# Small inputs spread over 128 partitions, w_out read in 8-KB runs, and the engines' work lists written anew

## The chip, the cores and the metric

The kernel runs on one core of one Trainium2 chip. The metric is the device time of one execution in microseconds (us). Before the change seven executions gave a median of 246.35 us, from 245.91 to 246.79. A measurement of this kernel can tell about 0.2% (0.5 us) from no change.

## The reference: what is computed

Inputs are q, k and v with 8 batches, 8 heads, 576 rows and 64 columns, p with 32 rows instead of 576, and the weights w_in (512 x 2048), w_out (2048 x 512) and beta (2048), all fp32.

```
sm_attn(q, k, v) = softmax(q k^T / 8) v
p_packed = sm_attn(p, k, v)              # 32 rows per head
x = sm_attn(q, p_packed, p_packed)       # 576 rows per head; heads side by side: 4608 x 512
h = x @ w_in                             # 4608 x 2048
out = (h * sigmoid(beta * h)) @ w_out    # 4608 x 512
```

## The kernel before

**The work.** Each batch b passes through two stages. The attention stage transposes k and q, forms the scores of p against k (`s1`, `s1r`), their exponentials (`e1`) and sums (`z1`), and the packed values `pp`. The second attention is never multiplied out: `scaled_w` (line 793, the instruction in 798) forms W = (pp times w_in) times 1/sum times beta, 128 rows by 2048 columns in two halves r, and the second attention's weights A2 (`s2`, `e2`, `z2`, `l2`, `n2`, `A2`) multiply W directly. The MLP stage forms h(b, ft) = W A2 for 16 blocks ft of 128 hidden columns (`main`), takes Silu on ScalarE (`g`), and multiplies by w_out (`o` tasks, in batches 0 and 1 plainly, from batch 2 on with seven products of half size, `p` and `P`). Because Silu is taken of beta times h, w_out is divided by beta row by row when it is cast to bf16 (`cast_out`, line 1276, tasks `w_out`).

**The layout that the change touches.** Hidden column f sits in block ft = f // 128 on partition f % 128. So w_out is loaded as `(f p) n -> p f n` (`load_out`, line 1270): for each of 128 partitions four rows of 2 KB, a quarter of w_out (1 MB) per load, four loads `ld_out` 0 to 3. beta is loaded as 16 rows of 128 (`load_beta`, 1143), made safe against division by zero (`safe`, 1220), transposed to a column per block (`column`, task `bcol`), inverted (`rbeta`), and spread to all partitions with fp32 matmuls (`spread`, tasks `brow`, then `beta`). p of batches 0 and 1 is loaded with 32 rows on 32 partitions (`load_first`, 1148), cast, transposed in four pieces (`first_transpose`, 1159) and placed; p of the other six batches is loaded later on 96 partitions (`load_p`, 1151), doubled and transposed (`transpose`, 1191; `place`, 1200).

**The order.** Nothing is scheduled when the program runs. `SEQUENCE` (line 54) lists, for TensorE (PE), ScalarE (ACT), VectorE (DVE), GpSimd (POOL) and SyncE (SP), the tasks in the order in which each engine issues them; every engine works through its own list and waits where an input is not there. `Planner.run` walks the five lists with an estimate for each task. The estimates move no task, but from them `fill` (in `run`) decides how many small matmuls without use (`keep_warm`, tile `o_ps<-identr`) stand in a place where PE is expected to wait during the first 60 us. SP issues nearly all the copies. In its list the loads of batches 0 and 1 and of the weights stand in one row, and each of the three staging buffers of w_in and w_out has to be cast before it is loaded again.

The places that the prediction's steps touch are these. `("o", 0, 1, 13)` is in both versions the first product that reads the last quarter of w_out; it needs `w_out` 12 and 13. Before it PE's list has

```
("s2", 0, 1), ("s2", 1, 0), ("o", 0, 1, 9), ("z2", 0, 2), ("o", 0, 0, 9), ("w", 1, 0), ("o", 0, 0, 11),
("z2", 1, 0), ("o", 0, 1, 11), ("o", 0, 1, 13), ("z2", 1, 1), ...
```

## Time and profile before

| what | value |
|---|---|
| median of 7 executions | 246.35 us |
| the profiled execution | 245.62 us, of which its span is 243.8 us |
| PE busy | 229.5 us (94%), 2432 matmuls, of them 147 without use (13.2 us) |
| ACT busy | 174.8 us (72%) |
| DVE busy | 153.7 us (63%) |
| POOL busy | 60.3 us (25%) |
| granted TensorE clock | 0.999 |
| DMA | 54.13 MB in 74986 packets, mean 222 GB/s |

The span runs from the first to the last recorded instruction of the core; 1.8 us of the execution lie around it. All times below that are given as points (51.37 us, say) are counted from the start of the span. A line of the timeline gives start, length, engine, source line, operation and tiles, and in brackets the idle time before it with what ended it. In the chain of work that ended last, each piece is followed back to what released it.

### The profile page before, as it was taken

What the parts mean: (1) busy time and instruction counts of PE and PEld (TensorE: products, weight loads), DVE (VectorE), ACT (ScalarE), POOL (GpSimd) and SP (SyncE); (2) the same over time, 40 slices, a digit from 0 to 9 for tenths busy, and PEclk for the clock granted to TensorE, in tenths of its full rate; (3) what the DMA queues carried; (4) which work ended last, traced back from release to release, by engine and by line L of the source; (5) the groups of instructions that cost most, each with busy time, mean ns of one, the idle gap of its engine ahead of it and who ended that gap; (6) DMA issues with size and microseconds to landing.
All of it is one profiled execution on the core that took longest, in us unless ns stands there. A gap on an engine that the chain in (4) does not pass through costs nothing.

```text
span 243.8 us, 5850 instructions
## 1 busy us (share of the span) xinstructions
PE 229.5 (94%) x2432; PEld 153.3 (63%) x2460; DVE 153.7 (63%) x244; ACT 174.8 (72%) x311; POOL 60.3 (25%) x77
## 2 busy tenths in 40 slices
PE   3997889989999999999999999999999999999994
PEld 3985545534464444687578754876588655767893
DVE  5445966879946636993798447845895158912721
ACT  2355969787797997797578866998798769866210
POOL 6422001125443065018520452036006000000000
PEclk9999999999999999999999999999999999999999
DMA  6999999999999999999999996998991530006033
GB/s 178 323 335 322 340 377 322 368 255 320 235 242 188 279 290 266 228 290 309 238 221 267 305 176 165 264 314 234 193 291 42 114 151 4 0 0 218 0 110 107
DMA packets 74986, 54.13 MB, mean 222 GB/s; under 512 B 42720, under 2 KB 68592, under 8 KB 74960
## 3 DMA queue, kind: packets, MB, share of 16 engines
q1 hardware_dynamic: 74496, 53.55, 84.8%
q8 instruction: 19, 0.31, 0.5%
q10 hardware_dynamic: 464, 0.21, 0.4%
q14 instruction: 7, 0.06, 0.1%
HBM read 37.23 MB, written 9.44 MB: 191 GB/s over the span
## 4 chain that ended last, share of the span: by engine, by line
PE 77%; DMA 14%; SPq 3%; DVE 2%; ACT 1%; issue 1%; DVEq 0%
PE o_ps L385 44%; PE h_ps L385 19%; DMA w_out<-in_moe_w_out_dram 5%; DMA w_in<-in_moe_w_in_dram 4%; DMA vr<-in_v_dram 4%; PE w_ps L385 3%; PE hr_ps L385 3%; DMA k<-in_k_dram 2%; SPq L445 2%; PE s_ps L385 2%; PE z_ps L385 2%; PE pp_ps L385 2%; DVE W_bf L798 1%; SPq L437 1%; ACT w_out_bf L1279 1%
## 5 line engine op out<-in xcount | busy, mean ns | idle before, releaser
L830 ACT ACTIVATE g_main<-h_ps 128x512 bf16<-128x512 f32 x128 | 72.4, 597 | 29.7 <-PE h_ps L385 24.6
L385 PE MATMUL o_ps<-w_out_bf,g_main 128*128 128x256 bf16 (+1 forms) x409 | 71.6, 304 | 1.5 <-DVE w_out_bf L1279 1.0
L385 PEld LDWEIGHTS <-g_main 128*128 128x128 bf16 x608 | 56.2, 98 | 26.5 <-issue 4.5
L385 PE MATMUL h_ps<-A2T,W_bf 128*128 128x512 bf16 x237 | 67.9, 379 | 0.9 <-ACT g_main L830 0.2
L798 DVE SCALAR_TENSOR_TENSOR W_bf<-w_ps,rz,beta_bc 128x512 bf16<-128x512 f32 x64 | 44.4, 745 | 10.7 <-PE w_ps L385 10.3
L385 PEld LDWEIGHTS <-W_bf 128*128 128x128 bf16 x512 | 32.8, 98 | 21.4 <-issue 5.4
L400 ACT ACT_TABLE_LOAD x24 | 30.8, 1283 | 1.1 <-PEq L1345 0.7
L466 POOL CAST q_bf<-q 128x1024 bf16<-128x1024 f32 x13 | 14.9, 1161 | 60.7 <-DMA q<-in_q_dram 47.8
L1060 DVE TENSOR_TENSOR o_sb<-o_ps,o_sb 128x512 f32<-128x512 f32 x18 | 12.4, 690 | 22.9 <-PE o_ps L385 18.7
L385 PE MATMUL o_ps<-w_sum,g_main 128*128 128x256 bf16 x192 | 25.4, 273 | 0.0
L385 PE MATMUL o_ps<-w_sum,g_sum 128*128 128x256 bf16 x192 | 24.0, 273 | 0.1
L385 PEld LDWEIGHTS <-g_sum 128*128 128x128 bf16 x192 | 18.3, 98 | 3.7
L466 POOL CAST v_bf<-v 128x1024 bf16<-128x1024 f32 x13 | 14.4, 1123 | 23.1 <-DMA v<-in_v_dram 20.4
L385 PE MATMUL o_ps<-identr 128*128 128x128 bf16 x147 | 13.2, 240 | 3.7 <-DVE bones L1125 3.7
L385 PE MATMUL o_ps<-w_out_bf,g_rem 128*128 128x512 bf16 (+1 forms) x78 | 16.5, 336 | 0.1
L1062 ACT COPY o_sb<-o_ps 128x512 f32<-128x512 f32 x13 | 7.6, 584 | 10.8 <-PE o_ps L385 10.8
L466 POOL CAST k_bf<-k 128x1024 bf16<-128x1024 f32 x12 | 12.3, 1042 | 11.5 <-DMA k<-in_k_dram 6.2
L385 PEld LDWEIGHTS <-identr 128*128 128x128 bf16 x147 | 10.8, 109 | 6.2 <-DVE bones L1125 3.7
L739 DVE TENSOR_TENSOR A2T<-E2T,rz 128x512 bf16<-128x512 bf16 x16 | 11.0, 699 | 2.9 <-ACT rz L734 2.9
L385 PE MATMUL w_ps<-w_in_bf,pp 64*32 64x512 bf16 x256 | 11.8, 383 | 0.9 <-DVE w_in_bf L1268 0.7
L385 PEld LDWEIGHTS <-pp 64*32 64x32 bf16 x384 | 4.1, 89 | 11.2 <-issue 8.3
L850 ACT ACTIVATE g_rem<-hr_ps 128x512 bf16<-128x512 f32 x16 | 9.6, 597 | 2.0 <-PE hr_ps L385 1.7
(102 smaller groups left out, 265.6 us busy)
## 6 DMA issues: line engine op xcount, KB each, us to landing
out_dram<-o_sb SPq DMA_DIRECT2D x14, 512.0 KB, 3.7
k<-in_k_dram SPq DMA_DIRECT2D x6, 1024.0 KB, 9.5
q<-in_q_dram SPq DMA_DIRECT2D x6, 1024.0 KB, 8.2
v<-in_v_dram SPq DMA_DIRECT2D x6, 1024.0 KB, 9.9
w_in<-in_moe_w_in_dram SPq DMA_DIRECT2D x4, 1024.0 KB, 9.1
w_out<-in_moe_w_out_dram SPq DMA_DIRECT2D x4, 1024.0 KB, 10.8
k<-in_k_dram SPq DMA_DIRECT2D x4, 512.0 KB, 9.0
q<-in_q_dram SPq DMA_DIRECT2D x4, 512.0 KB, 7.4
```

The costliest lines, as they stand in the source:

```text
L385: return self.nc.tensor.matmul(out, lhsT, rhs, start=start, stop=stop, tile_position=pos, skip_group_check=True)
L400: self.nc.scalar.preload_act_table_set(SETS[mode])
L437: nc.sync.dma_start(t[:, 0:2048].rearrange("p (h e) -> p h e", h=8)[:, h], src[b, h, 0:SM, :].rearrange("h (p t) d -> p h (t d)", p=128),)
L445: nc.sync.dma_start(t[64 * g : 64 * g + 64, :].rearrange("p (h d) -> p h d", h=4), src[b, 4 * g : 4 * g + 4, SM:S, :].rearrange("h p d -> ...
L466: self.copy[engine](o[:, 0:2048].rearrange("p (t h d) -> p h t d", t=4, h=8)[:, h], t[:, 0:2048].rearrange("p (h t d) -> p h t d", h=8, t= ...
L739: nc.vector.tensor_tensor(part(st[b, "A2"], i), part(st[b, "E2"], i), st[b, "rz2"][:, i] if i < 2 else st[b, "rz2r"][:], ALU.mult)
L798: nc.vector.scalar_tensor_tensor(st[b, "W"][:, r, cols], st[b, "w", m][:], st[b, "rz1"][:, r : r + 1], self.beta_bc[:, cols], op0=ALU.mult ...
L830: nc.scalar.activation(st[b, "g"][:, ft, :], st[b, "h", ft][:], AF.Silu)
L850: nc.scalar.activation(st[b // 2, "gr"][:, 8 * half : 8 * half + 8, o : o + 64], st[b, "hr", half][:].rearrange("p (f n) -> p f n", f=8), ...
L1060: nc.vector.tensor_tensor(o, x, o, ALU.add)
L1062: self.copy[engine](o, x)
L1279: nc.vector.tensor_scalar_mul(o, w, r) if engine == "DVE" else nc.scalar.mul(o, w, r)
```

## The change

There are three parts, and the lists.

1. **p in 128 partitions.** p of batches 0 and 1 is loaded as 4 pairs of heads by 32 rows on 128 partitions, in two copies (one for each head of a pair) of 128 runs of 256 B, instead of one copy of 256 such runs on 32 partitions. The cast is then 128 x 128 instead of 32 x 512, and one transpose takes the place of four. The later load takes p of all eight batches, 128 partitions of 4 KB instead of 96; the doubling, the 16 transposes and the placing work on 128 rows, and the first two batches are dropped when the result is placed.
2. **w_out in 8-KB runs.** Partition p takes rows 4p to 4p+3 of a quarter. Hidden column 512n + 4p + f is then in block 4n + f on partition p, so the columns of W are permuted when they are scaled: the input is read from PSUM with a step of four elements, the output is contiguous, and beta's row lies permuted already.
3. **beta in 4 rows of 512.** One fp32 matmul of 512 columns with 4 rows of weights replaces four of 128 columns in each `brow`; `bcol` becomes four small transposes. The buffer for this is the second buffer of `g`, so the first `h` of batch 1 now also waits for `brow` 3 and `bcol`.
4. **The lists.** All five are written anew, and some tasks change the engine. No task is added or taken out. Useless matmuls number 134 instead of 147.

```diff
-                st[b, "W"][:, r, cols], st[b, "w", m][:], st[b, "rz1"][:, r : r + 1], self.beta_bc[:, cols],
+                st[b, "W"][:, r, cols].rearrange("q (f p) -> q f p", f=4),
+                st[b, "w", m][:].rearrange("q (p f) -> q f p", f=4),
+                st[b, "rz1"][:, r : r + 1],
+                self.beta_bc[:, cols].rearrange("q (f p) -> q f p", f=4),
...
-        oldg = self.users(b - 2)
+        oldg = self.users(b - 2) + [("brow", 3), ("bcol",)] * (b == 1)
...
-            self.b16 = self.sm.tile([16, 128], f32, tag="rz1", name="b16")
-            nc.scalar.dma_start(self.b16[:], self.beta.rearrange("(f p) -> f p", p=128))
+            self.b4 = self.spare()[0:4, 0:512]
+            nc.scalar.dma_start(self.b4, self.beta.rearrange("(n j) -> n j", n=4))
...
-            self.p0[b] = t = self.sm.tile([32, H, D], f32, tag="E2T", name="p0")
-            (nc.sync if b else nc.scalar).dma_start(t[:], self.p[b].rearrange("h s d -> s h d"))
+            self.p0[b] = t = self.sm.tile([128, 2, D], f32, tag="E2T", name="p0")
+            pair = self.p[b].rearrange("(c r) s d -> c s r d", r=2)
+            for r in range(2):
+                (nc.sync if b else nc.scalar).dma_start(t[:, r], pair[:, :, r])
...
-            nc.sync.dma_start(self.p32[0:LATER], self.p[PE_BATCHES:B].rearrange("b h (a s) d -> (b h a) s d", s=16))
+            nc.sync.dma_start(self.p32[:], self.p.rearrange("b h (a s) d -> (b h a) s d", s=16))
...
-            for c in range(NC):
-                self.tp(ps[:, 32 * c : 32 * c + 32], self.p0_bf[b][:, 128 * c : 128 * c + 128], self.identr[0:32, 0:32])
+            self.tp(ps[:, 0:128], self.p0_bf[b][:], self.identr[:])
...
-            for i in range(4):
-                f = 4 * n + i
-                self.mm(
-                    self.br[:, 128 * i : 128 * i + 128],
-                    self.ident32[:, f : f + 1].to_broadcast([128, 128]),
-                    self.b_safe[:],
-                )
+            self.mm(
+                self.br[:].rearrange("q (f p) -> q f p", f=4),
+                self.ident32[0:4, n : n + 1].to_broadcast([4, 128]),
+                self.b_safe.rearrange("n (p f) -> n f p", f=4),
+            )
...
-                t[:], self.w_out[512 * n : 512 * n + 512, :].rearrange("(f p) n -> p f n", p=128)
+                t[:], self.w_out[512 * n : 512 * n + 512, :].rearrange("(p f) n -> p f n", p=128)
```

In the lists, what bears on the start is this. SP's order up to the last quarter of w_out was k0 (first half), p1, q0, q0, v0, k0 and its rest, w_in 0, v0 and its rest, w_in 1, the rest of q0, k1, k1, w_out 0, the rest of k1, w_in 2, w_out 1, v1, w_in 3, q1, v1 and its rest, q1, w_out 2, w_out 3 (the digit is the batch, or the quarter of a weight). It becomes k0, p1 (two copies), q0, k0 and its rest, q0, v0, v0 and its rest, w_in 0, w_in 1, w_out 0, k1, k1 and its rest, w_in 2, w_out 1, the rest of q0, w_in 3, q1, q1, v1, v1 and its rest, w_out 2, w_out 3. The same loads stand ahead of `ld_out` 3 in both. The cast of the first half of k0 moves from DVE to POOL, behind that of p; `b_safe` moves from POOL to the head of DVE's list. Before the first reader of the last quarter of w_out, PE's list now has

```
("s2", 0, 1), ("s2", 1, 0), ("w", 1, 0), ("o", 0, 1, 9), ("o", 0, 0, 9), ("o", 0, 1, 11), ("z2", 1, 0),
("z2", 0, 2), ("z2", 1, 1), ("o", 0, 0, 11), ("o", 0, 1, 13), ...
```

so that `("z2", 1, 1)` is the only task that has crossed that place. `w_out` 13 moves from DVE to ACT, behind `("e2", 1, 1)`, and `w_out` 14 and 15 from ACT to DVE. In the tail, PE ends with the same last three tasks, and DVE with the same last two.

## The prediction, as it was put on record

> **What bounds the kernel now.** I read the page's busy shares and its 40 slices first, then the chain of work that ended last, then PE stretch by stretch. From the page:

> ```profile
> PE 229.5 (94%) x2432; PEld 153.3 (63%) x2460; DVE 153.7 (63%) x244; ACT 174.8 (72%) x311; POOL 60.3 (25%) x77
> ...
> PE   3997889989999999999999999999999999999994
> ...
> DMA  6999999999999999999999996998991530006033
> ```

> PE is full from about the ninth slice on, DMA from the second. So the kernel has two regimes, and the chain in order of time says where one gives way to the other:

> ```profile
> 22.86 9.48 DMA w_in<-in_moe_w_in_dram
> ...
> 39.52 11.83 DMA w_out<-in_moe_w_out_dram
> 51.37 1.34 ACT w_out_bf L1279 x2
> ...
> 53.24 0.86 PE o_ps L385 x4
> ```

> Up to 51.35 us the chain lies mostly in loads; the last of them is the last quarter of w_out. After that it is PE almost without a break. PE's timeline shows the hand-over:

> ```profile
> 52.31 0.38 PE L385 MATMUL o_ps<-w_out_bf,g_main 128*128 128x512 bf16 x1 [1.01 <-DVE w_out_bf L1279]
> ```

> This is the first product on the last quarter of w_out. PE had waited 1.01 us for its cast. From there the busy times by stretch:

> ```profile
> 60.00:100.00 40.00, 39.58 (x391) 19.73 (x396) 25.86 (x41) 33.77 (x59) 15.54 (x18) 1.00 1.11 247
> 100.00:140.00 40.00, 39.64 (x479) 29.67 (x483) 28.84 (x42) 31.51 (x59) 13.08 (x15) 1.00 1.08 271
> 140.00:180.00 40.00, 39.74 (x439) 26.21 (x443) 26.45 (x39) 32.51 (x56) 10.67 (x13) 1.00 1.04 225
> 180.00:220.00 40.00, 39.68 (x384) 27.41 (x387) 22.85 (x34) 31.66 (x60) 4.22 (x5) 1.00 0.24 73
> 220.00:236.20 16.20, 16.20 (x159) 13.80 (x157) 6.79 (x7) 5.45 (x11) 0.00 (x0) 1.00 0.33 115
> ```

> The second column is PE: it idles 0.3 to 0.4 us in 40, at the full clock (the 1.00). New lists have nothing to win there; they can only lose. So the time is a sum of four: the hand-over at 52.31, PE's work behind it up to 240.2 (187.9), the last eviction and store (3.6), and 1.8 around the span: 245.6, the profiled execution, which is 0.7 below the median of 246.35. I work out the change of this sum and put it on the median.

> **What moves the hand-over: the loads.** The same loads stand ahead of the last quarter of w_out in both orders of SP, and DMA has no gap there, so only their cost counts.

> *w_out in 8-KB runs.* By the trace's packet records up to 52 us, a 256-B packet takes 18 ns, one of 1 KB 46 to 51, one of 2 KB 84 to 88; a 4-KB store later takes 160. That is a line of 8 ns plus 38 ns per KB, so 8 KB would take 312 against four times 86 = 344. Each of 16 DMA engines has 8 such runs per quarter: 8 x 32 ns = 0.26 us, four quarters 1.0. With the ends of those rows it is 0.8 to 1.3. There is a row that says otherwise: p's 96 loads of 4 KB took 297 ns, not 160. If that came from the length of the run, 8 KB would take 600 and each quarter 2.0 us more, 8.2 in all. But those loads use 96 partitions, and their bytes are few; the 2-KB loads of 128 partitions are nearer. I take -1.0 and keep +8.2 as an end.

> *p of batches 0 and 1.* Bytes and run length stay (512 runs of 256 B for the two batches), so with an even split the cost stays at 32 packets per engine, 0.6 us: 0. All copies of the trace post 16 completions each, none shows an uneven split. The other end: the source pattern of the new copies has 4 pairs as its outermost count, where it had 32 rows. If the engines are dealt out by that count, 4 of 16 carry all, 128 packets instead of 32, and 96 x 18 ns = 1.7 us later for every load behind that needs them; the other twelve are 0.6 earlier. How much of it reaches the landing depends on a skew that is there already. The sixteen completions of the last quarter of w_out come at 48.29 (first), 48.91 (median), 50.95, 51.18 and 51.35. Three engines lag by 2.0 to 2.4 us, since each was held by one of the 16-KB instruction fetches at 14.65, 24.55 and 39.70 (1.05 to 1.11 us each), of which the page counts 19, 0.31 MB in all:

> ```profile
> q8 instruction: 19, 0.31, 0.5%
> ```

> If the four engines are others than these three, their 1.7 hides behind the 2.4, and the landing is even 0.6 earlier. If one is in both, the landing is 1.7 later.

> [...]

> *The place itself.* In before two casts follow one another on DVE (51.37 to 52.25). In the new lists w_out 12 on DVE (0.48) lies beside w_out 13 on ACT (0.72): -0.2. One task, z2 of 0.22 us, now lies before the hand-over, in idle time: -0.2. The limit is the chain ahead: z2(1, 1) waits for the exponential e2(1, 1), which ended at 50.24, now stands behind one more cast on ACT (0.72), but starts from v of batch 1, which lands 0.5 earlier by two quarters of w_out. So z2 at 50.5, one product (0.43), and the hand-over at 51.1 to 51.2 at the earliest: -1.2, whatever DMA gives.

> **What does not reach the sum.** *W's strided read* is done 64 times, so its price matters most. By form, on DVE:

> ```profile
> L798 DVE SCALAR_TENSOR_TENSOR W_bf<-w_ps,rz,beta_bc 128x512 bf16<-128x512 f32 x64 | 44.4, 745 | 10.7 <-PE w_ps L385 10.3
> ...
> L1062 DVE COPY o_sb<-o_ps 128x512 f32<-128x512 f32 x11 | 7.6, 689 | 5.3 <-PE o_ps L385 5.2
> ...
> L1202 DVE COPY pT<-pT_ps 64x384 bf16<-64x384 bf16 x2 | 1.0, 558 | 0.0
> ```

> The plain fp32 copy of 512 elements takes 689 ns and the one of 256 elements (L897) 424, so 1.04 ns per element and 158 fixed. L1202 reads PSUM in steps of 192 B, and 384 x 1.04 + 158 = 557: the step costs nothing beyond one element per step, the pace W has already. I take 0. The other end is two steps per element, 0.53 us x 64 = 34 us on an engine with 90 us free; behind the hand-over, from 52.3 to 60, DVE is busy 7.2 of 7.7 us, so the four W there would cost PE about 2 us, and all of them perhaps 4. [...]

> *Before the first h* (27.57) PE fills its waits with useless matmuls, 124 of the 147 by then, so what happens there has cover: k0's cast on POOL (1.04 against 0.77 us, behind p's), b_safe on DVE (three operations of 512 elements, about 0.7 each, before kT's eviction), two more issues of p (0.5 each on ACT and on SP), four fp32 columns more or less. If that cover were gone it would be some 2 us on the first scores; but v now lands some 3 us earlier (w_in 0, 2.75 us between landings, goes behind it), so pp is not later. The new wait of h(1, *) for brow 3 and bcol is for tasks that PE's own list has before the first h; it is over by order. *The later p* brings 128 runs of 4 KB for 96 behind w_out, +0.3 us of DMA at 160 ns or +0.6 at 297, where PE has a backlog: 0. Its 16 transposes take 56 instead of 42 ns: +0.2. Its placing moves from ACT to DVE (2 x 0.56), where DVE is busy 13.9 of 20 us: 0. *The tail* has the same last three products and last two evictions: 0.

> **Sum:** loads -1.0, casts -0.2, z2 -0.2, transposes +0.2, cut off at -1.2 by the chain: -1.0 to -1.2. 246.35 - 1.05 = 245.3.

> **Rivals.**
> *A, the uneven split (the other side).* The place is the landing of w_out 3, the price 1.7 - 1.0 - 0.2 = +0.5 to +0.7, and it decides as soon as one of the four engines is one of the three that lag. For it: the count 4 in the pattern, and a landing that is set by the slowest engine already. Against it: twelve engines are relieved. 246.9.
> *B, the chain takes it all.* The loads come earlier but e2(1, 1) and its z2, which now stand before the hand-over, are late: with v of batch 1 moved behind q, one half-load (1.5 us) of slip there eats the gain. 246.2.
> *C, long runs or strides are slow.* +2 to +8: 248.5 to 254.5. For it: the 297 ns of p; against it: L1202 and the line through three sizes.
> *D, the lists lose in the full stretch.* Every engine's order is new behind the hand-over; one stall of 0.3 us per batch is 2 us, 248. Against it: before's lists have none.

> **How the numbers follow.** Forecast 0.42 (own range 244.3, where DMA gives 1.3 and 0.6 more and the chain moves with it, to 246.0), A 0.28 (246.3 to 247.6), B 0.15, C 0.07, D 0.08. Within 0.2% (0.5 us, what a measurement of this kernel can tell) lie most of B, a third of A and a tenth of the forecast: 0.25. Faster: the rest of the forecast and a little of B, 0.42. Slower: 0.33. The range leaves out C and the edges: 244.3 to 248.0.

> **What would show it.** Right: the last quarter's cast starts near 50.3, the first product on it at 51.1, PE's work behind it is 187.9 +- 0.3. Packets of 8 KB at 312 ns. Wrong: the sixteen completions spread wider than 2.4 us from the start (A); e2 and z2 ahead of the cast as the releaser of that product (B); L798 over 760 ns or packets over 350 (C); PE idle over 0.6 us in a stretch of 40 (D).

## The result, and the profile after

The changed kernel takes 249.62 us (median of 12 executions, 248.16 to 251.16), the kernel before beside it 246.15 us (31 executions): the ratio is 1.0134 with a 95% interval from 1.0114 to 1.0154. The forecast was 245.3. The profiled execution of the changed kernel took 248.18 us, one of the quicker of its twelve. A ratio is not the quotient of two medians and can differ a little from it (1.0081 and 1.0110 for before_brow4 below); the one slow execution among the runs below, of c128_p16, is left out of its ratio.

The page of the changed kernel, its busy shares and its slices (6.2 us each):

```profile
PE 236.2 (96%) x2392; PEld 153.7 (62%) x2420; DVE 156.4 (63%) x243; ACT 173.4 (70%) x309; POOL 68.1 (28%) x79
...
PE   4999999999999999999999999999999999999993
...
PEclk9975799999999999999999999999999999999999
DMA  6999799999999999999599959996992430104024
```

PE is now full from the second slice on, where before had digits under 9 up to the ninth, and it is busier by 6.7 us for a span that is 2.5 longer. The change was to add hardly any work to PE, so PE must be slower somewhere: the row PEclk has 7, 5, 7 in slices 3 to 5, where before had 9 in all forty. DMA has a hole in slice 5: SP had waited 5.2 us for a cast of w_in on DVE, whose buffer the third quarter of w_in needs, when it issued that load at 26.83. Here are the stretches of 6 us of the start, before and after (PE is the second column, the granted clock the third from the end):

```profile
6.00:12.00 6.00, 6.00 (x82) 5.85 (x80) 2.91 (x6) 1.86 (x4) 2.61 (x4) 1.00 1.11 328
12.00:18.00 6.00, 5.71 (x88) 5.33 (x86) 3.10 (x7) 3.78 (x8) 1.56 (x1) 1.00 1.07 328
18.00:24.00 6.00, 4.49 (x73) 3.13 (x69) 3.50 (x8) 2.74 (x7) 1.56 (x1) 1.00 1.10 321
24.00:30.00 6.00, 4.58 (x52) 3.01 (x54) 5.37 (x10) 5.87 (x9) 0.10 (x1) 1.00 1.07 338
```

```profile
6.00:12.00 6.00, 5.57 (x42) 3.46 (x41) 4.75 (x7) 1.47 (x3) 2.20 (x4) 0.94 1.11 305
12.00:18.00 6.00, 6.00 (x49) 3.77 (x47) 2.31 (x5) 1.54 (x5) 2.44 (x3) 0.78 1.09 317
18.00:24.00 6.00, 6.00 (x49) 3.46 (x47) 1.80 (x6) 1.83 (x3) 1.04 (x1) 0.51 1.03 393
24.00:30.00 6.00, 6.00 (x64) 3.60 (x63) 2.93 (x6) 4.65 (x8) 1.04 (x1) 0.64 0.76 226
```

From 12 to 24 us PE is recorded as busy without a break and has the clock at 0.78 and 0.51; the idle time that before had there (1.8 us of 12) is gone, and the matmuls in it are fewer. By the clock records the half clock stood from 11.25 to 14.66 and from 18.08 to 28.32 us, 13.7 us in all. What PE did then is in the chain of work that ended last:

```profile
2.57 3.64 DMA x<-in_moe_beta_dram
...
8.91 2.04 PE brow_ps L384 x2
10.95 1.41 PE o_ps L384 x15
12.37 0.85 PE kT_ps L389 x8
...
14.29 2.07 PE brow_ps L384 x2
...
17.38 1.97 PE brow_ps L384 x2
...
22.40 2.07 PE brow_ps L384 x2
```

Each `brow` takes 2 us. Two rows, of groups by form, show what changed in it; first before, then after (busy us in all, mean ns of one; the 16 fp32 matmuls of before left 32 records here, the 4 of after 8):

```profile
L385 PE MATMUL brow_ps<-b_safe,ident 128*128 128x128 f32 x32 | 4.5, 283 | 0.0
```

```profile
L384 PE MATMUL brow_ps<-x,ident 4*128 4x512 f32 x8 | 8.4, 1131 | 0.3 <-DVE x L1233 0.3
```

That is 3.9 us more on PE, of the 6.7.

The first h comes at 31.24 us instead of 27.57 (before, then after):

```profile
27.57 0.81 PE L385 MATMUL h_ps<-A2T,W_bf 128*128 128x512 bf16 x3
```

```profile
31.24 1.10 PE L384 MATMUL h_ps<-A2T,W_bf 128*128 128x512 bf16 x3
```

The hand-over, the first product on the last quarter of w_out, is the third product of the second group in these lines of PE's timeline (behind the two of `("o", 0, 0, 11)`, 0.22 us each), at 54.40 us:

```profile
53.75 0.38 PE L384 MATMUL z_ps<-E2T,bones 128*128 128x512 bf16 x1
53.97 1.89 PE L384 MATMUL o_ps<-w_out_bf,g_main 128*128 128x512 bf16 x7
```

There is no bracket with an idle time: PE waits for no load there, it is late by itself. The last quarter is issued at 41.43 instead of 39.52 and lands at 52.50, later than the 51.35 of before, but the casts of its first two blocks are done at 54.14, ahead of PE.

The four terms of the prediction's sum, profiled execution against profiled execution: hand-over 54.40 against 52.31, +2.1; PE's work behind it (its end 242.53) 188.1 against 187.9, +0.3; last eviction and store, and what lies around the span, +0.1 each. That is the 248.18 - 245.62 = 2.56 by which the two executions differ. The rest of the span runs at the full clock, as before:

```profile
60.00:100.00 40.00, 39.58 (x394) 20.09 (x395) 25.75 (x40) 33.40 (x57) 18.81 (x21) 1.00 1.13 255
...
180.00:220.00 40.00, 39.63 (x408) 27.48 (x411) 24.54 (x35) 32.02 (x60) 3.32 (x4) 1.00 0.32 87
```

### The profile page after: what moved, and what is told of

Its sections match the earlier page's. It is cut to its first block, busy times and chain, and to the rows that moved or that the text cites. A ratio compares the mean times of both kernels' runs of the same rounds, so it can differ in the third digit from the quotient of the medians.

```text
span 246.3 us, 5782 instructions
## 1 busy us (share of the span) xinstructions
PE 236.2 (96%) x2392; PEld 153.7 (62%) x2420; DVE 156.4 (63%) x243; ACT 173.4 (70%) x309; POOL 68.1 (28%) x79
## 3 DMA queue, kind: packets, MB, share of 16 engines
q1 hardware_dynamic: 72984, 53.68, 80.6%
## 4 chain that ended last, share of the span: by engine, by line
PE 89%; DVE 4%; ACT 2%; DMA 1%; issue 1%; ACTq 0%
PE o_ps L384 47%; PE h_ps L384 21%; PE w_ps L384 4%; PE brow_ps L384 3%; PE hr_ps L384 3%; PE s_ps L384 2%; PE pp_ps L384 2%; PE z_ps L384 2%; DMA x<-in_moe_beta_dram 1%; PE qT_ps L389 1%; ACT L399 1%; DVE A2T L743 1%; PE kT_ps L389 1%; DVE g_main L1037 1%; DVE o_sb L1069 1%
## 5 line engine op out<-in xcount | busy, mean ns | idle before, releaser
L384 PEld LDWEIGHTS <-g_main 128*128 128x128 bf16 x608 | 56.8, 98 | 24.2 <-issue 2.5
L384 PE MATMUL o_ps<-w_out_bf,g_main 128*128 128x256 bf16 (+1 forms) x409 | 69.1, 304 | 0.7 <-DVE o_sb L1069 0.2
L465 POOL CAST q_bf<-q 128x1024 bf16<-128x1024 f32 x14 | 18.1, 1310 | 40.4 <-DMA q<-in_q_dram 34.4
L384 PE MATMUL o_ps<-w_sum,g_sum 128*128 128x256 bf16 x192 | 24.8, 273 | 0.1
L465 POOL CAST v_bf<-v 128x1024 bf16<-128x1024 f32 x15 | 17.9, 1205 | 23.8 <-DMA v<-in_v_dram 14.0
L465 POOL CAST k_bf<-k 128x1024 bf16<-128x1024 f32 x14 | 14.9, 1073 | 17.1 <-DMA k<-in_k_dram 14.8
L1069 DVE COPY o_sb<-o_ps 128x512 f32<-128x512 f32 x15 | 10.3, 685 | 7.0 <-PE o_ps L384 7.0
L743 DVE TENSOR_TENSOR A2T<-E2T,rz 128x512 bf16<-128x512 bf16 x16 | 12.6, 792 | 2.5 <-ACT rz L738 2.3
L702 ACT ACTIVATE E2T<-s_ps,rz 128x512 bf16<-128x512 f32 x16 | 10.3, 685 | 1.4 <-PE s2r_ps L384 0.7
```

Of the source, the lines that this page charges most:

```text
L384: return self.nc.tensor.matmul(out, lhsT, rhs, start=start, stop=stop, tile_position=pos, skip_group_check=True)
L465: self.copy[engine](o[:, 0:2048].rearrange("p (t h d) -> p h t d", t=4, h=8)[:, h], t[:, 0:2048].rearrange("p (h t d) -> p h t d", h=8, t= ...
L702: nc.scalar.activation(st[b, "E2"][:, i, 0:SM], st[b, "s2", i][:], AF.Exp, scale=st[b, "rz1"][:, 2 + i : 3 + i])
L743: nc.vector.tensor_tensor(part(st[b, "A2"], i), part(st[b, "E2"], i), st[b, "rz2"][:, i] if i < 2 else st[b, "rz2r"][:], ALU.mult)
L1069: self.copy[engine](o, x)
```

## The experiments

**Theory 1:** the four `brow` matmuls lower PE's clock while the start is on PE, and the whole of the start is late by it. Three forms of it: the step of four elements in the moving operand does it, the four rows do it, or the step makes the length and the rows the clock (1c). **Rival 2:** p and beta come on fewer DMA engines (their copies post 5 completions each, all others 16; that this means four engines is the author's estimate), so the start is late. **Rival 3:** the new lists.

All edits are to the changed kernel, unless they say "before". The variants of `brow`:

contig4 permutes beta as it is made safe, so that it is read contiguously:

```diff
-            e.tensor_tensor(x, b, b, ALU.mult)
+            x3, b3 = x.rearrange("n (f p) -> n f p", f=4), b.rearrange("n (p f) -> n f p", f=4)
+            e.tensor_tensor(x3, b3, b3, ALU.mult)
...
-                self.b_safe.rearrange("n (p f) -> n f p", f=4),
+                self.b_safe,
```

stride128 keeps the step and takes 128 rows of weights and of x, 124 of them zeros:

```diff
+            nc.gpsimd.memset(self.spare()[:, 1024:1536], 0.0)
...
-                self.ident32[0:4, n : n + 1].to_broadcast([4, 128]),
-                self.b_safe.rearrange("n (p f) -> n f p", f=4),
+                self.ident32[:, n : n + 1].to_broadcast([128, 128]),
+                self.spare()[:, 1024:1536].rearrange("n (p f) -> n f p", f=4),
```

contig128 does both. contig4x2 and contig128x2 are contig4 and contig128 with each of the four matmuls issued twice.

*contig4.* 

> Edit: beta is permuted as it is made safe, so that spread and column read it contiguously; still 4 rows of weights. Theory 1 (brow: the four spreading matmuls of 2.04 us stand in PE's list and half the clock until 28.3; the step of four elements in their moving operand makes both): brow falls to about 1.0 us, the clock stays at 1.0 in 12 to 28 us, the first h comes at 27.5 to 28.5, time 245.3 to 246.8. Theory 1b (the few rows make both): brow stays at 2.0, clock 0.5, time 248 to 250. Theory 1c (the step makes the length, the four rows the clock): brow 1.0 while the clock is full, but the clock still falls, time 247 to 249. Rival 2 (DMA: p and beta on four engines start late) and rival 3 (the new lists): 248 to 250 whatever brow does.

*contig128.* 

> Edit: as contig4, and the spreading matmuls use 128 rows, of which 124 are zeros from one POOL memset. Theories 1, 1b and 1c: brow 1.0, clock 1.0 throughout, first h at 27.5 to 28.5, time 245.3 to 246.8; between 1 and the others it tells nothing. Rivals 2 and 3: 248 to 250 with the clock at 1.0 as well.

*stride128.* 

> Edit: the step of four elements stays, but the spreading matmuls use 128 rows, of which 124 are zeros from one POOL memset. Theory 1: no change from after: brow 2.0, clock 0.5 from 11 to 28 us, time 248 to 250. Theory 1b: brow 1.0, clock 1.0, 245.3 to 246.8. Theory 1c: brow 2.0 (1.0 us longer four times), clock 1.0, first h at 28 to 30, time 246.5 to 248. Rivals 2 and 3: 248 to 250.

Measured (the clock is the median over all executions of the mean granted clock; beside these runs the kernel before had 0.997 to 0.999; brow is from the profiled execution):

| kernel | rows | step | PE busy in brow, us | clock | ratio to before |
|---|---|---|---|---|---|
| after | 4 | yes | 8.4 | 0.966 | 1.0134 [1.0114, 1.0154] |
| contig4 | 4 | no | 4.7 | 0.971 | 1.0089 [1.0051, 1.0128] |
| contig4x2 | 4 | no | 11.6 | 0.963 | 1.0263 [1.0227, 1.0299] |
| stride128 | 128 | yes | 8.1 | 0.995 | 1.0020 [0.9991, 1.0049] |
| contig128 | 128 | no | 4.4 | 0.993 | 1.0045 [1.0015, 1.0074] |
| contig128x2 | 128 | no | 7.8 | 0.999 | 1.0014 [0.9991, 1.0036] |

The groups by form of contig4 and of stride128:

```profile
L384 PE MATMUL brow_ps<-x,ident 4*128 4x512 f32 x8 | 4.7, 672 | 1.7 <-DVE x L1234 1.7
```

```profile
L384 PE MATMUL brow_ps<-x,ident 128*128 128x512 f32 x8 | 8.1, 1100 | 1.0 <-DVE x L1234 1.0
```

Form 1c holds. The step makes the length (stride128 is as long as after, contig4 as short as contig128), and the rows make the clock: with the step and 128 rows, nearly all of the loss is gone. In time, contig4 and contig128 are not told apart by themselves (their intervals overlap), and contig128 at 247.37 us lies above the 246.8 that was expected at most; what is left there is taken up with p16 and the lists below. Rivals 2 and 3 fall as the main cause, since these kernels keep the copies and the lists. The step matters only through the time that PE spends on four rows, and two more kernels test just that.

*contig4x2.* 

> Edit: contig4 (beta contiguous, 4 rows), each spreading matmul issued twice, so that PE spends some 2.1 us per brow without any step. If a step in the moving operand matters only through the time that PE spends in matmuls of 4 rows (theory 1c made exact): clock low as in after, 1.0 to 1.5% over before. If the step itself lowers the clock: as contig4, 0.6 to 1.1% over before.

*contig128x2.* 

> Edit: contig128 (beta contiguous, 128 rows), each spreading matmul issued twice, some 2.1 us per brow. Theory 1c: the length alone has cover, the clock stays at 1.0: as stride128 and contig128, 0.1 to 0.5% over before. Rival (the length of brow in the start is what costs, by whatever clock): 1.0 to 1.5% over before.

They differ in the rows alone (and one memset), and are 6.25 us apart: medians of 252.59 and 246.34. The rows PEclk of their pages, contig4x2 and then contig128x2:

```profile
PEclk9766779999999999999999999999999999999998
```

```profile
PEclk9999999999999999999999999999999999999998
```

So 3.4 us more of spreading on PE cost nothing that could be told (contig128x2 against contig128): the length has the cover that the prediction gave it. The same matmuls on 4 rows cost 2.6%. More was lost here than the upper bound of 1.5% in the expectation, since the half clock lengthened the spreading itself: one task of this kernel, its matmul twice, took 1.98 us at the full clock and 3.75 at the half one.

```profile
17.14 1.98 PE L384 MATMUL brow_ps<-x,ident 4*128 4x512 f32 x4
...
20.06 3.75 PE L384 MATMUL brow_ps<-x,ident 4*128 4x512 f32 x4
```

*before_brow4*, the other way round: the cause put into the kernel before.

```diff
-            for i in range(4):
-                f = 4 * n + i
-                self.mm(
-                    self.br[:, 128 * i : 128 * i + 128],
-                    self.ident32[:, f : f + 1].to_broadcast([128, 128]),
-                    self.b_safe[:],
-                )
+            self.mm(
+                self.br[:].rearrange("q (f p) -> q f p", f=4),
+                self.ident32[0:4, n : n + 1].to_broadcast([4, 128]),
+                self.x4.rearrange("n (p f) -> n f p", f=4),
+            )
```

> Edit: the kernel before with its sixteen spreading matmuls of 128 x 128 replaced by four of 4 rows and 512 columns read with a step of four elements, out of a tile of ones (beta is left out of W). Theory 1c: each brow takes 2.0 to 2.1 us instead of 1.0, the clock falls to 0.5 for 3 to 14 us between 9 and 25 us, the first h comes at 29 to 31 instead of 27.6, time 1 to 3 us above before. Rival (the lists of after, not brow, take the cover away): the clock stays at 1.0 and the time within 0.5 of before.

248.78 us, ratio 1.0081 [1.0048, 1.0115], median clock 0.971. In its profile (249.59 us) the half clock lasts from 11.77 to 28.84 us, longer than expected, and the first h comes at 33.35, later than expected:

```profile
PEclk9955699999999999999999999999999999999999
```

With before's lists, p and w_out, the four matmuls (with one memset and one more wait of batch 1's first h) bring most of the loss back, 0.8% of 1.3%. Over all sixteen kernels, the five with 4-row matmuls have median clocks of 0.963 to 0.971, the others 0.991 to 1.000, whatever else they do.

*p16*: p of the first batches by rows, so that the copies post 16 completions each instead of 5.

```diff
-            pair = self.p[b].rearrange("(c r) s d -> c s r d", r=2)
+            pair = self.p[b].rearrange("(c r) s d -> s c r d", r=2)
...
-                self.p0_ps[b][h, 0 : 32 * NC].rearrange("p (c s) -> p c s", c=NC),
+                self.p0_ps[b][h, 0 : 32 * NC].rearrange("p (s c) -> p c s", c=NC),
```

> Edit: p of batches 0 and 1 is put into the 128 partitions row by row instead of pair by pair, so that the source's outermost count is 32 and the copies use 16 engines; brow as in after. Theory 1 and its kinds: 248 to 250, brow 2.0, clock as in after. Rival 2 (p and beta on four engines): the first k0, q0 and beta land 0.5 to 1.5 us earlier, first h at 29 to 30, time 246.5 to 248. Rival 3 (lists): 248 to 250. The number of completions goes up by 44 (four copies of 16 for four of 5).

249.76 us, ratio 1.0163 [1.0100, 1.0225], clock 0.971: no gain, so rival 2 falls while the clock is low. The same edit with `brow` mended is c128_p16 (contig128 and p16 together):

> Edit: contig128 (beta contiguous, 128 rows in the spreading matmuls), and p of batches 0 and 1 row by row, so that its copies run on 16 engines. Theory 1c (the clock and brow are all of the loss of the start; the uneven split of p then sets when w_out lands): the clock is 1.0, the four engines' lag of 1.1 to 1.4 us behind the median at the first loads goes to 0.5 or less, the last quarter of w_out lands 0.5 to 1.2 us earlier than the 52.16 of contig128, time 246.2 to 247.0 (contig128: 247.4). Rival (other lags set the landing, or the time behind it is set elsewhere): no change, 247.0 to 247.8.

246.44 us, ratio 1.0005 [0.9977, 1.0033]. The clock is full, and the hand-over is close to where the forecast had put it, 51.1 to 51.2:

```profile
51.32 1.60 PE L384 MATMUL o_ps<-w_out_bf,g_main 128*128 128x512 bf16 x5 [0.26 <-DVE w_out_bf L1287]
```

Yet it is no faster than before: PE's work behind the hand-over is 189.07 us here, 187.86 there. And that the 16 completions instead of 5 made the difference to contig128 is not shown: the last completion's lag behind the median in the loads that land from 6 to 10 us did not shrink as expected (1.1 to 1.6 us in both), and c128_p16_late96 below, with the same loads up to w_out, landed at 52.30 us against 50.75 here.

*before_w8 and c128_w2*: the run length of w_out alone, put into before and taken out of contig128 (the same lines the other way round).

```diff
-                t[:], self.w_out[512 * n : 512 * n + 512, :].rearrange("(f p) n -> p f n", p=128)
+                t[:], self.w_out[512 * n : 512 * n + 512, :].rearrange("(p f) n -> p f n", p=128)
```

> Edit: the kernel before with w_out loaded in 8-KB runs and nothing else; the row order does not match the columns of W. By the forecast: the last quarter lands at 50.4 instead of 51.35, hand-over at 51.2 to 51.4, time 0.8 to 1.1 below before. Rival (hidden): within 0.3 of before.

> Edit: contig128 with w_out loaded in 2-KB runs as in before; the row order of w_out then does not match the columns of W, so the product is of other rows. By the forecast's price (8 KB 312 ns against four times 86): the last quarter lands 1.0 us later than in contig128 (52.2), 53.2, time 248.0 to 248.5. Rival (the run length is hidden by lags and by other packets): 247.0 to 247.8.

before_w8 takes 245.72 us, ratio 0.9977 [0.9960, 0.9994]: the 8-KB runs do gain, about half of the forecast. The last quarter lands at 50.88 instead of 51.35, the hand-over is at 51.84, and PE's wait for it falls from 1.01 to 0.44 us:

```profile
51.84 0.38 PE L385 MATMUL o_ps<-w_out_bf,g_main 128*128 128x512 bf16 x1 [0.44 <-DVE w_out_bf L1279]
```

c128_w2 has 1.0043 [1.0021, 1.0064] where contig128 has 1.0045: nothing to be told there, though in its profile the last quarter lands at 53.68 (expected 53.2), 1.5 us after that of contig128.

*mended_oldlists*: all parts mended as in c128_p16, with before's five lists. *old_w8*: before's lists and p, and of the change only w_out, W and beta, mended as in contig128.

> Edit: c128_p16 (all of the change, with beta contiguous and in 128 rows and p on 16 engines), but with the five lists of the kernel before. If the new lists cost the 1.0 to 1.2 us that lie behind the hand-over in c128_p16 (189.1 against 187.9): time 0.3 to 0.6% under before. If they do not: as c128_p16, 0.3% either way of before. b_safe is then on POOL, where it takes some 3 us.

> Edit: the kernel before with its own lists and its own p, and of the change only w_out in 8-KB runs, W permuted, and beta in 4 rows made contiguous and spread with 128 rows. What before_w8 gained (0.2%) less what b_safe of 512 elements on POOL costs the start: 0.0 to 0.3% under before. If the permuted read of W costs on DVE: over before.

They have 1.0039 [1.0014, 1.0065] and 0.9994 [0.9974, 1.0014]. With the same parts, the old lists are not better than the new (1.0005). And old_w8, with W's columns permuted, is not over before.

*c128_p16_late96*: c128_p16 with the later p, its doubling and its transposes as in before.

```diff
-            nc.sync.dma_start(self.p32[:], self.p.rearrange("b h (a s) d -> (b h a) s d", s=16))
+            nc.sync.dma_start(self.p32[0:LATER], self.p[PE_BATCHES:B].rearrange("b h (a s) d -> (b h a) s d", s=16))
```

*old_w8_dve*: old_w8 with `b_safe` moved from POOL to DVE, as it looked the best version.

```diff
-        ("p0_bf", 0), ("b_safe",), ("p0_bf", 1), ("w_in", 0, 1), ...
+        ("p0_bf", 0), ("p0_bf", 1), ("w_in", 0, 1), ...
...
-        ("cast", 0, "k", 0), ("cast", 0, "q", 0), ("rbeta",), ...
+        ("cast", 0, "k", 0), ("b_safe",), ("cast", 0, "q", 0), ("rbeta",), ...
```

> Edit: c128_p16 with the later load of p, its doubling and its transposes on 96 rows, as in before. If the later p is what lies behind the hand-over (PE waits 0.4 us for p_dup there, and 16 transposes are 14 ns longer): PE's work behind the hand-over falls from 189.1 by 0.4 to 0.6, time 0.1 to 0.3% under before. If it is something else: as c128_p16, within 0.1% of its ratio of 1.0005.

> Edit: old_w8 with b_safe on DVE, behind the cast of the first half of k0, instead of POOL. PE's wait of 1.4 us for b_safe ahead of bcol goes down, but the cast of q0 and the placing of k stand 2.6 us later on DVE. If the start before the first h still has cover for it: 0.2 to 0.4% under before. If not: the first h comes 0.5 to 1.5 us later than the 27.0 of old_w8, and the time is 0.1% under to 0.3% over before.

c128_p16_late96 has 1.0046 [1.0027, 1.0065]: the later p is not what lies behind the hand-over (PE still waits 0.6 us for its doubling there, and 188.7 us follow the hand-over). That it is slower than c128_p16 was in neither expectation; in its profile the hand-over comes 1.5 us later, at 52.86, and a stretch at half clock stands in the start. old_w8_dve has 0.9981 [0.9961, 1.0001], 245.85 us against 246.29: the lowest ratio of the versions that compute everything, and not told apart from before with certainty. The first h comes 0.7 us later than in old_w8 (27.69 against 27.01), so the start had not all of the cover.

## Why the prediction was wrong, step by step

**The step that failed** is in "Before the first h": "so what happens there has cover: ... four fp32 columns more or less". That is all that the prediction says of the spreading: a length on an engine with idle time, put at nothing in the sum. The length was indeed longer and had cover (contig128x2). But the prediction took the clock of 1.00 in before's rows as given, and the useless matmuls as mere filling. Four rows of weights put PE at half clock for 13.7 us of the start, which lengthened most of PE's work there, useful or not: in the median a useless matmul took 314 ns instead of 219, a transpose of k the same, and one of the products of `s2` 605 instead of 386. The next sentence gave "some 2 us on the first scores" if the cover were gone: it was 3.7 us at the first h, 2.1 at the hand-over, and 3.5 in the medians. No rival named the clock; the range ended at 248.0.

**What bounds the kernel** was right for before and moved by the change: the loads, which ended last at 51.35, no longer do. PE does, from 8.9 us on, but for 28.5 to 32.9 us, where the chain lies mostly in DVE (W, A2 and casts). Nor did "DMA has no gap there, so only their cost counts" hold for the changed kernel: slice 5 is a gap. DVE's list has the cast that SP waits for behind `rbeta`, and `rbeta` waits 2.85 us for `bcol`, which PE comes to only at 25.28; so the slow PE held up the loads too.

**w_out in 8-KB runs.** The price was right: in before_w8 the packets have medians of 313 to 314 ns (312 forecast) and means of 321 to 332. The sum was too large: -1.0 became -0.5 at the landing and 0.23% of the time. The rival of 600 ns is out. In the changed kernel one quarter's packets are slower than the line has them, 341 ns in the median for the third.

**p on four engines (A).** The completions show an uneven split: the changed kernel posts 2057, 127 times 16 and five times 5 (of each five, one at 2.19 to 3.42 us and four at 4.21 to 6.41), before 130 times 16. The five are the four copies of p and that of beta (c128_p16, with p by rows, has one left); before's trace has no such copy. How many engines carried those copies no run shows: the four of sixteen, dealt out by the pattern's outermost count, and with them the 1.7 us of the price, were the author's estimate. What the split costs is not settled. Nor is it shown that instruction fetches made the skew: in before four completions lag, not three (50.74 too), and no record says which engine a fetch was on.

**Casts and z2; B.** c128_p16 hands over at 51.32, near the cut at 51.1 to 51.2, but by another wait than the prediction's: z2(1, 1) started at 50.24, earlier than the 50.5 of the prediction, and PE waited for the cast, whose load landed at 50.75 instead of about 50.3. That the numbers are so near is in part luck.

**W's strided read (C).** Right: 0.

```profile
L802 DVE SCALAR_TENSOR_TENSOR W_bf<-w_ps,rz,beta_bc 128x512 bf16<-128x512 f32 x64 | 44.7, 744 | 15.1 <-PE w_ps L384 14.9
```

744 ns against 745 before, the 64 times with a step of four.

**Work behind the hand-over, 187.9.** Right for the changed kernel (188.1), wrong as a constant. It was 188.6 to 189.1 us in c128_p16, stride128, contig128 and contig4, which hand over at 51.3 to 53.2, and 187.9 and 188.2 in before_brow4 (before's work) and contig4x2, at 56.3 and 58.3; but p16, at 55.6, has 189.0, and old_w8, at 51.5, has 188.3. So some of an earlier hand-over may be given back; that is not shown. Waits that the trace names (0.4 us for the doubling of p, 0.2 for an eviction) are half of the 1.2 us in c128_p16; the rest stays open.

**D, the lists.** Not supported by mended_oldlists.

## What to carry to other kernels

A matmul on four rows was not cheap filling here (median clocks of 0.963 to 0.971 in the five kernels whose spreading runs on four rows, 0.991 to 1.000 in the eleven others, whose spreading runs on 128; what lies between was not tried): ask of each small one in a stretch where PE hides other work whether the granted clock stays up, for the drop slowed most of what stood behind it, fillers too (314 ns instead of 219). Read PEclk beside PE: the fuller PE was the slower one here (6.00 of 6.00 us busy at a clock of 0.51). And a gain at a hand-over is a gain at the end only as far as the work behind it is ready as early.
